# Splits of w_v and w_r made during the routed attention, parked in DRAM, and casts of x moved to ScalarE

## The chip, the core and the metric

The kernel runs on one core of a Trainium2 chip. Its engines are TensorE (PE, with the weight loads shown apart as PEld), VectorE (DVE), ScalarE (ACT) and GpSimd (POOL); SyncE (SP) issues most transfers between DRAM and the on-chip memory SBUF. Each engine works through its own queue in order; semaphores make it wait for others. The metric is the device time of one execution in microseconds (us), lower is better.

## The reference

Three stages follow each other: attention in a local window with a few global tokens (4 batches, 8 heads, 512 local and 32 global tokens, 64 wide), a mixture of 4 attention experts of which each token takes 2, and a channel mix:

```python
x_prev = concat([zeros, x[:, :-1]], axis=1)
xk = mu_k * x + (1.0 - mu_k) * x_prev
xr = mu_r * x + (1.0 - mu_r) * x_prev
k = maximum(xk @ w_k, 0.0)          # w_k is 512 x 1024
v = k * k @ w_v                     # w_v is 1024 x 512
r = 1.0 / (1.0 + exp(-(xr @ w_r)))  # w_r is 512 x 512
return r * v
```

The tokens are 4 x 576, 512 wide. Inputs of w_k, w_v and w_r arrive as 64-bit floats, so that each needs bit work before TensorE can take it.

## The kernel before, in words

A product of two fp32 matrices is made of three matmuls on a high and a low part of each operand (`mm3`). Activations and weights are therefore *split*: a cast gives the high part H, a subtraction the low part L.

The first 32 steps (n = 0 to 31) are the local attention; from step 33 on the routed attention's steps m = n - 33 run beside its end, and afterwards alone, up to m = 38 (`c_step`). A batch takes nine of them: two pairs of heads with four query blocks each, and one step for the global rows. Within a step come, in a pipeline over m, m - 1, m - 2 and m - 3, the scores (`C`, L101), their softmax on DVE and ACT (`csm`, L483 and L485), the normalisation on POOL (L501), the transposes on TensorE (`cT`, L510) with their copies out by ACT (L513) and DVE (L515, `cpt`), and the product with the values (`y`, L581). Between these, `fill` hands out groups of the projections of the next batch (`pv`, `pb..q`, `pb..k`), which need x split (`b_split`, cast L364 on DVE, subtraction L365 on POOL), and of the output projections (`po`) of the batch before.

Behind the routed attention comes the channel mix, in units of 256 tokens: mixing (`mtr`, `mmr`, `m..H`, `m..L`), eight column blocks f of `k`, each squared and split (`ksr`, `k2r`, `kk`), then `v` and `r`, and the output. Its first four blocks of `k` are made during the last batch.

The weights of the channel mix come in pieces of 128 rows x 512 columns: eight of w_k, eight of w_v (four in each half `wv0`, `wv1`), four of w_r. `load_wd` loads a piece's 512 KB into one of two `raw` buffers. `split_wd` turns it into H and L: on ACT the sign and the absolute value (L133, L134), on POOL a maximum (L136), on DVE three bit operations (L138 to L140), on ACT the cast to H (L141), on POOL the subtraction to L (L142). Its two work tiles are `wg` and `wy`, two buffers of each. H and L are written straight into tiles that earlier work uses before: w_v's first half takes the buffers of the projections' weights (`W0`, `W1`), its second half and w_r's H the `qk` buffers of the last batch, w_r's L those of w_o.

Before the change, w_k's pieces are loaded and split in steps m = 7, 10, ... 28 and the next, w_v's first half from m = 31 on, every second step, and the other eight pieces in a row behind the last output projection. w_o is split at m = 7. The order on every engine is set by a scheduler that goes by the program's order and its own estimate of when things are ready; `after(...)` keeps an instruction from being placed ahead of a given one.

## Time and profile before

| | |
|---|---|
| device time, median of 3 runs (lowest to highest) | 588.25 us (585.49 to 590.0) |
| the profiled execution: its time, its span | 588.06 us, 586.3 us |
| busy: PE, PEld | 551.9 us (94%), 458.9 us (78%) |
| busy: DVE, ACT, POOL | 342.2 us (58%), 331.1 us (56%), 315.6 us (54%) |
| mean granted clock of TensorE | 0.971 of full speed |
| moved between DRAM and SBUF | 38.72 MB, 66 GB/s over the span |

A row of the profile names a line of the kernel, an engine, an operation, and the tiles as out<-in. "Idle before" is the time in which the engine did nothing ahead of an instruction, and "<-" what ended it. Matmuls overlap, so a sum of their durations is more than their time; the distance of their starts is what counts. The granted clock is the share of TensorE's full speed that it was given in a stretch. The busy shares above are means over stages with different limits.

### The profile page before, as it was taken

How to read it: one execution, taken by the hardware profiler on the slowest of the kernel's cores; microseconds unless marked ns; L12 is line 12 of the kernel's file. 1: busy time of each engine (PE TensorE's matmuls, PEld its weight loads, DVE VectorE, ACT ScalarE, POOL GpSimd, SP SyncE). 2: the span in 40 equal slices, each digit the busy share in tenths (PEclk: the TensorE clock that was granted, in tenths of full speed). 3: DMA queues.
4: the chain of work that ended last, by engine and by line, in shares of the span. 5: the costliest groups of instructions: out<-in, count | busy, mean ns of one | idle time of the engine just before them, and what ended most of it. 6: DMA issues, size and time to landing. Idle time of an engine off the chain costs nothing. (4 is left out here: it accounts for less than half of the span.)

```text
span 586.3 us, 12786 instructions
## 1 busy us (share of the span) xinstructions
PE 551.9 (94%) x4670; PEld 458.9 (78%) x4670; DVE 342.2 (58%) x1153; ACT 331.1 (56%) x995; POOL 315.6 (54%) x416
## 2 busy tenths in 40 slices
PE   4999999999899998999998955999999999999997
PEld 2767787789788886888787833889898989898896
DVE  3768666664677487458788888864342434224211
ACT  5788775653365554365797766575444554344321
POOL 2778635352446475355688999854444443334121
PEclk9899999999899997899999986999999999999999
DMA  8998523020002110111113223000000100000000
GB/s 321 309 299 236 179 76 109 2 92 2 2 2 73 36 36 2 37 37 37 37 37 108 73 72 108 1 36 37 2 37 0 37 1 36 3 36 26 12 19 36
DMA packets 19918, 38.72 MB, mean 66 GB/s; under 512 B 9616, under 2 KB 10640, under 8 KB 19856
## 3 DMA queue, kind: packets, MB, share of 16 engines
q1 hardware_dynamic: 19280, 37.50, 19.6%
q8 instruction: 37, 0.61, 0.4%
q10 hardware_dynamic: 576, 0.41, 0.2%
q14 instruction: 25, 0.20, 0.1%
HBM read 33.45 MB, written 4.46 MB: 65 GB/s over the span
## 5 line engine op out<-in xcount | busy, mean ns | idle before, releaser
L675 POOL TENSOR_TENSOR kk<-k2r,kk 128x256 fp32r<-128x256 f32 x64 | 51.0, 800 | 78.4 <-ACT kk L674 78.4
L672 DVE TENSOR_TENSOR k2r<-ksr 128x256 f32<-128x256 f32 x64 | 34.4, 537 | 78.5 <-ACT ksr L671 74.6
L501 POOL TENSOR_TENSOR csm<-csm,crc 128x128 f32<-128x128 f32 (+3 forms) x64 | 48.7, 781 | 45.7 <-DVE crc L498 14.5
L222 ACT ACTIVATE sm<-sm,mn 128x160 f32<-128x160 f32 x128 | 53.4, 419 | 20.4 <-DVE mn L219 19.6
L655 DVE SCALAR_TENSOR_TENSOR mmr<-xT,mu,mtr 128x256 f32<-128x256 f32 (+4 forms) x96 | 52.0, 581 | 14.2 <-POOL m1L L659 6.5
L485 ACT ACTIVATE csm<-csm,cmn 128x128 f32<-128x128 f32 (+3 forms) x64 | 35.7, 559 | 30.7 <-DVE cmn L483 25.6
L671 ACT ACTIVATE ksr<-k 128x256 f32<-128x256 f32 x64 | 24.1, 379 | 44.4 <-PE k L95 44.3
L659 POOL TENSOR_TENSOR m1L<-mmr,m1H 128x256 fp32r<-128x256 f32 (+1 forms) x36 | 26.8, 757 | 32.0 <-ACT m1H L658 31.9
L654 ACT ACTIVATE mtr<-xT,omu 128x256 f32<-128x256 f32 (+4 forms) x96 | 39.7, 440 | 5.9 <-DVE mmr L655 5.1
L674 ACT CAST kk<-k2r 128x256 fp32r<-128x256 f32 x64 | 25.8, 404 | 27.4 <-DVE k2r L672 25.3
L240 POOL TENSOR_TENSOR pn<-sm,rc 128x256 f32<-128x256 f32 x64 | 37.9, 615 | 3.9 <-PE pT L259 3.0
L219 DVE CUSTOM_DVE_ANT_0 sm<-S,band 128x160 f32<-128x160 f32 x128 | 34.1, 317 | 7.3 <-PE S L209 6.3
L581 PE MATMUL y<-cpt,vC 128*64 128x128 f32 (+1 forms) x320 | 36.1, 306 | 0.7 <-DVE gsl L428 0.5
L209 PE MATMUL S<-kq 64*64 64x160 f32 x512 | 32.3, 323 | 4.3 <-DMA kq<-in_kq_dram 4.0
L93 PE MATMUL v<-wv1H,kk 128*128 128x512 f32 x68 | 27.4, 415 | 6.9 <-ACT wv1H L141 6.9
L510 PE MATMUL cT<-ident,csm 128*128 128x128 f32 x160 | 29.0, 295 | 4.7 <-DVE cpt L515 2.3
L94 PE MATMUL v<-wv1L,kk 128*128 128x512 f32 x68 | 28.1, 413 | 5.5 <-POOL wv1L L142 5.5
L244 POOL TENSOR_TENSOR glob<-sm,rc 128x128 f32<-128x128 f32 x32 | 13.0, 406 | 37.4 <-DVE rc L236 26.0
L483 DVE CUSTOM_DVE_ANT_0 csm<-C,causal 128x128 f32<-128x128 f32 (+3 forms) x64 | 29.3, 484 | 3.4 <-PE C L101 3.3
L720 DVE TENSOR_TENSOR o<-v,rt 128x512 f32<-128x512 f32 x17 | 11.6, 685 | 32.4 <-PE v L95 15.3
L365 POOL TENSOR_TENSOR x<-xT,x 128x256 fp32r<-128x256 f32 (+1 forms) x32 | 24.0, 777 | 11.9 <-DVE x L364 11.9
L581 PEld LDWEIGHTS y<-cpt,vC 128*64 128x64 f32 x320 | 22.0, 140 | 10.2 <-issue 6.0
(408 smaller groups left out, 1907.7 us busy)
## 6 DMA issues: line engine op xcount, KB each, us to landing
kq<-in_kq_dram SPq DMA_DIRECT2D x15, 688.0 KB, 4.8
vw<-in_vw_dram SPq DMA_DIRECT2D x16, 512.0 KB, 5.6
out_dram<-o SPq DMA_DIRECT2D x17, 256.0 KB, 2.0
wrawk<-in_moe_w_k_dram SPq DMA_DIRECT2D x8, 512.0 KB, 3.6
wrawv<-in_moe_w_v_dram SPq DMA_DIRECT2D x8, 512.0 KB, 3.6
wrawr<-in_moe_w_r_dram SPq DMA_DIRECT2D x4, 512.0 KB, 3.5
vgb<-in_vgd_dram SPq DMA_DIRECT2D x1, 512.0 KB, 8.3
rawwq<-in_moe_wq_dram SPq DMA_DIRECT2D x4, 128.0 KB, 9.3
```

Of the source, the lines that this page charges most:

```text
L209: nc.tensor.matmul(st[h][64 * c:64 * c + 64, i * W:(i + 1) * W], t[rr, 64 * blk:64 * blk + 64], t[rr, KT0 + 96 * blk:KT0 + 96 * blk + W], ...
L219: last_dve = nc.vector.tensor_tensor_reduce(out=ts[:, h, i], in0=st[h][:, i * W:(i + 1) * W], in1=band[:, m], op0=ALU.add, op1=ALU.min, sc ...
L222: last_act = nc.scalar.activation(ts[:, h, i], ts[:, h, i], AF.Exp, bias=mn[:, c:c + 1], scale=-1.0, accum_out=su[:, c:c + 1])
L240: nc.gpsimd.tensor_tensor(o[:, :, c], t[:, :, 96 * c:96 * c + 64], rc[:, :, None].to_broadcast([128, 4, 64]), op=ALU.mult)
L483: nc.vector.tensor_tensor_reduce(out=t[:, :w], in0=st[e][:, :w], in1=causal[:, 512 - w:], op0=ALU.add, op1=ALU.min, scale=-SCALE, scalar=B ...
L485: last_act = nc.scalar.activation(t[:, :w], t[:, :w], AF.Exp, bias=mn[:, e:e + 1], scale=-1.0, accum_out=su[:, e:e + 1])
L501: last_pool = nc.gpsimd.tensor_tensor(t[:, :w], t[:, :w], rc[:, e:e + 1].to_broadcast([128, w]), op=ALU.mult)
L581: nc.tensor.matmul(yp[64 * e:64 * e + 64, o0:o0 + n], vC[b][:, j, hh * HD:(hh + 1) * HD], pt[:, e, j, 0:n], start=j == 0, stop=j == i and ...
L654: nc.scalar.mul(mt[:, cc], xp, omu[:, kind, c:c + 1])
L655: nc.vector.scalar_tensor_tensor(mm[:, cc], x, mu[:, kind, c:c + 1], mt[:, cc], op0=ALU.mult, op1=ALU.add)
L672: nc.vector.tensor_mul(k2, s, s)
L675: nc.gpsimd.tensor_sub(hl[1], k2, v32(hl[0]))
```

## The change

1. A *jobs* list now holds w_o's load and split, then the eight pieces of w_v, the four of w_r and the eight of w_k. From m = 1 on, two of each three steps load one piece, and a split follows a step or so later; the last is done at about m = 32.
2. The pieces of w_v and w_r are split in place: H goes into the tile `wg`, L into `wy`, and both are written to a scratch in DRAM (`dr`), 256 KB each.
3. `fetch_wd` loads whole halves back into the places where they were before: w_v's first half and the H of its second at m = 30, the L of its second at m = 34, w_r behind the last output projection. A fetch is 1 MB, or two of 512 KB where the place has two buffers.
4. The cast of x in `b_split` stays on DVE for the first batch and goes to ACT for the other three.

The operations of a split, its shapes and the matmuls are the same.

```diff
-V0, VS = 31, 2
+J0, F0, F1 = 1, 30, 34
...
+    dr = ctx.enter_context(tc.tile_pool(name="dr", bufs=1, space=bass.MemoryType.DRAM))
...
+    wdr = {(name, k, s): dr.tile([128, 4, 512], F32, name=f"d{name}{k}{s}")
+           for name, k in (("v", 0), ("v", 1), ("r", 0)) for s in "HL"}
+
+    def place_wd(name, k, s):
+        tag = WD_TAG[name, k]["HL".index(s)]
+        m = 2 if tag == "wo" else 4
+        ts = [T(tag, [m, 512], f"w{name}{k}{s}{i}", F32R) for i in range(4 // m)]
+        wd.setdefault((name, k), []).append([t[:, j] for t in ts for j in range(m)])
+        return ts
+
+    def fetch_wd(name, k, s):
+        c = 0
+        for t in place_wd(name, k, s):
+            m = t.shape[1]
+            nc.sync.dma_start(v32(t), wdr[name, k, s][:, c:c + m])
+            c += m
...
+        if name == "k":
...
+            H_, L_ = [t[c % 4] for t in wd[name, k]]
+        else:
+            H_, L_ = g.bitcast(F32R), y.bitcast(F32R)
         nc.scalar.copy(H_, v32(y))
         nc.gpsimd.tensor_sub(L_, v32(y), v32(H_))
+        if name != "k":
+            for s, t in zip("HL", (H_, L_)):
+                nc.sync.dma_start(wdr[name, k, s][:, c % 4], v32(t))
...
-            nc.vector.tensor_copy(hl[0][:, c, :n], x)
+            (nc.vector.tensor_copy if b == 0 else nc.scalar.copy)(hl[0][:, c, :n], x)
...
-        if V0 <= m < V0 + 4 * VS and (m - V0) % VS == 0:
-            c = (m - V0) // VS
-            pending.append(load_wd("v", w_v, c, c // 4, 0))
-        if m >= 7 and (m - 7) % 3 == 0 and (m - 7) // 3 < 8:
-            k = (m - 7) // 3
-            pending.append(load_wd("k", w_k, k % 4, k // 4, 512 * (k // 4)))
-        if len(pending) > 1 or m >= V0 + 4 * VS - 1:
+        if jobs and m >= J0 and (m - J0) % 3 < 2:
+            pending.append(jobs.pop(0)())
+        if len(pending) > 1 or not jobs:
             for g in pending[:1]:
                 g()
             del pending[:1]
+        if m == F0:
+            for s in "HL":
+                fetch_wd("v", 0, s)
+            fetch_wd("v", 1, "H")
+        if m == F1:
+            fetch_wd("v", 1, "L")
...
+    jobs = [lambda: load_wo()]
+    jobs += [lambda c=c: load_wd("v", w_v, c, c // 4, 0) for c in range(NF)]
+    jobs += [lambda c=c: load_wd("r", w_r, c, 0, 0) for c in range(NC)]
+    jobs += [lambda c=c: load_wd("k", w_k, c % 4, c // 4, 512 * (c // 4)) for c in range(2 * NC)]
...
-    for g in pending:
-        g()
-    for c in range(4, NF):
-        load_wd("v", w_v, c, c // 4, 0)()
-    for c in range(NC):
-        load_wd("r", w_r, c, 0, 0)()
+    for s in "HL":
+        fetch_wd("r", 0, s)
```

How the change moves instructions is shown at three places. In these rows a tile's number tells copies of a tile apart, and line numbers of the changed kernel are up to 21 higher.

POOL behind the last output projection: `wy..` is a split's work tile, `w..L` a low part, `kk` and `m..` belong to the channel mix. Before:

```order
L142 TENSOR_TENSOR wv1L_5016<-wyv_5017,wv1H_5015 128x512
L136 TENSOR_SCALAR wyv_5029<-wyv_5029 128x512
L675 TENSOR_TENSOR kk<-k2r,kk 128x256
L659 TENSOR_TENSOR m0L_5117<-mmr,m0H_5116 128x256 x2
L136 TENSOR_SCALAR wyv_5041<-wyv_5041 128x512
L675 TENSOR_TENSOR kk<-k2r,kk 128x256
L142 TENSOR_TENSOR wv1L_5016<-wyv_5029,wv1H_5015 128x512
L675 TENSOR_TENSOR kk<-k2r,kk 128x256
L659 TENSOR_TENSOR m1L_5135<-mmr,m1H_5134 128x256 x2
L142 TENSOR_TENSOR wv1L_5016<-wyv_5041,wv1H_5015 128x512
L136 TENSOR_SCALAR wyv_5053<-wyv_5053 128x512
L659 TENSOR_TENSOR m1L_5135<-mmr,m1H_5134 128x256 x2
```

In the changed kernel, from the first blocks of `kk` after the routed attention on:

```order
L696 TENSOR_TENSOR kk<-k2r,kk 128x256 x2
L680 TENSOR_TENSOR m1L_4816<-mmr,m1H_4815 128x256 x4
L680 TENSOR_TENSOR m0L_5156<-mmr,m0H_5155 128x256 x4
L696 TENSOR_TENSOR kk<-k2r,kk 128x256
L680 TENSOR_TENSOR m1L_5174<-mmr,m1H_5173 128x256 x2
L696 TENSOR_TENSOR kk<-k2r,kk 128x256
L680 TENSOR_TENSOR m1L_5174<-mmr,m1H_5173 128x256 x2
L696 TENSOR_TENSOR kk<-k2r,kk 128x256
L680 TENSOR_TENSOR m_5379<-mmr,m_5379 128x256 x2
L696 TENSOR_TENSOR kk<-k2r,kk 128x256
L680 TENSOR_TENSOR m_5379<-mmr,m_5379 128x256 x2
```

The steps of the splits are gone from between the mixing and `kk`.

DVE at the cast of the fourth batch's x (`xT_87` and in the changed kernel `xT_89` are its rows; `cpt` is the copy of the transposed weights of attention), before:

```order
L385 TENSOR_TENSOR qk_2952<-pb21q_3561,qk_2952 128x288
L498 TENSOR_TENSOR crc_3623<-crc_3623,gate_2715 128x2
L364 CAST x_3629<-xT_87 128x256 x4
L515 COPY cpt_3595<-cT_3600 128x2x128
L385 TENSOR_TENSOR qk_2952<-pb21k_3580,qk_2952 128x288
L393 TENSOR_TENSOR ql<-pb21q_3561,ql 64x32
L483 ISA csm_3617,cmn_3607<-C_3609,causal 128x128
```

DVE in the changed kernel at the same copy, `128x2x128`, of the same step:

```order
L519 TENSOR_TENSOR crc_3733<-crc_3733,gate_2741 128x2
L150 SCALAR_TENSOR_TENSOR wgr_3706<-wrawr_3621,wgr_3706 128x512
L536 COPY cpt_3691<-cT_3696 128x2x128
L406 TENSOR_TENSOR qk_3016<-pb21q_3657,qk_3016 128x288
L504 ISA csm_3727,cmn_3717<-C_3719,causal 128x128
L504 ISA cmn_3717 128x1
L504 ISA csm_3730,cmn_3717<-C_3720,causal 128x128
```

And ACT in the changed kernel there:

```order
L405 CAST qk_3016<-pb21q_3657 128x288
L159 CAST wgr_3624<-wyr_3623 128x512
L405 CAST qk_3016<-pb21k_3676 128x288
L385 CAST x_3739<-xT_89 128x256 x3
L534 COPY cpt_3691<-cT_3692 128x2x128
L385 CAST x_3739<-xT_89 128x256
L413 CAST ql<-pb21q_3657 64x32
```

The four casts have left DVE, where they stood ahead of `cpt`; on ACT three of them stand ahead of its own half of that copy, and a step of a split of w_r (`wgr`) stands among the others on both engines.

SP in the changed kernel, around the first fetches (`wv1H<-dv1H` is a fetch, `wrawk` a load of a piece of w_k):

```order
L133 DMA wrawk_4167<-in_moe_w_k_dram 128x1024
L133 DMA wrawk_4352<-in_moe_w_k_dram 128x1024
L133 DMA wrawk_4432<-in_moe_w_k_dram 128x1024
L127 DMA wv1H_4663<-dv1H 128x2048
L127 DMA wv0H_4659<-dv0H 128x2048
L127 DMA wv0L_4661<-dv0L 128x2048
L133 DMA wrawk_4526<-in_moe_w_k_dram 128x1024
L133 DMA wrawk_4582<-in_moe_w_k_dram 128x1024
L133 DMA wrawk_4725<-in_moe_w_k_dram 128x1024
L127 DMA wv1L_4956<-dv1L 128x2048
L127 DMA wr0H_5147<-dr0H 128x2048
L127 DMA wr0L_5149<-dr0L 128x1024
```

Before, SP had one load behind the other there, and no write or fetch. Now three fetches of 1 MB stand ahead of the last three loads of w_k.

## Rows read from the trace of the kernel before

**Rows 1.** Busy time of each engine by stretch (start:end, length, busy us with the count of instructions for PE, PEld, DVE, ACT and POOL, then TensorE's granted clock, the DMA share and GB/s): the four batches of the routed attention, the stretch behind it, the rest.

```profile
130.00:172.00 42.00, 39.67 (x389) 34.74 (x387) 25.91 (x123) 18.95 (x59) 15.88 (x25) 0.96 0.01 2
172.00:222.00 50.00, 49.18 (x394) 40.94 (x393) 35.45 (x130) 28.25 (x83) 30.87 (x36) 1.00 0.13 43
222.00:272.00 50.00, 47.13 (x343) 39.17 (x342) 30.67 (x109) 25.03 (x72) 25.30 (x33) 0.90 0.07 22
272.00:322.00 50.00, 48.53 (x397) 38.48 (x396) 41.56 (x130) 38.88 (x111) 38.28 (x43) 1.00 0.20 64
340.00:382.00 42.00, 28.06 (x137) 21.73 (x136) 35.39 (x47) 27.71 (x68) 39.22 (x32) 0.80 0.21 63
382.00:586.00 204.00, 200.54 (x1161) 177.00 (x1159) 73.47 (x139) 89.48 (x239) 75.59 (x104) 1.00 0.06 23
```

**Rows 2.** TensorE's waits from 322 to 386 us: who waited for whom, us in total, times, longest.

```profile
PE v L93 <- ACT wv1H L141: 6.9, 3, 3.5
PE v L94 <- POOL wv1L L142: 5.5, 4, 3.0
```

**Rows 3.** The chain of waits from 338 to 382 us, shares by line.

```profile
by line: DVE wgr L139 11.9%; DVE mmr L655 9.3%; POOL wyv L136 8.4%; POOL wv1L L142 8.2%; POOL kk L675 8.2%; DVE wyr L140 7.6%; DVE wyr L138 7.5%; issue 7.2%; DVE wyv L140 5.1%; POOL m0L L659 4.6%; DVE wyv L138 4.2%; POOL wyr L136 3.7%; POOL
```

**Rows 4.** Busy time from 340 to 382 us of the instructions that touch `v`, then `k`, then `r` (columns as in rows 1, engines that have none left out).

```profile
340.00:382.00 42.00, 10.30 (x24) 5.44 (x24) 0.00 (x0) 0.80 0.21 63
...
340.00:382.00 42.00, 12.78 (x90) 12.55 (x88) 3.28 (x9) 0.80 0.21 63
...
340.00:382.00 42.00, 7.12 (x23) 4.16 (x24) 0.00 (x0) 0.80 0.21 63
```

**Rows 5.** TensorE in order of time (start, duration, line): two neighbours of `v`, and two of `k`, in undisturbed stretches.

```profile
387.68 0.39 PE L93 MATMUL v<-wv0H,kk 128*128 128x512 f32 x1
387.90 0.39 PE L94 MATMUL v<-wv0L,kk 128*128 128x512 f32 x1
...
338.03 0.28 PE L93 MATMUL k<-m,wk1H 128*128 128x256 f32 x1
338.15 0.28 PE L94 MATMUL k<-m,wk1H 128*128 128x256 f32 x1
```

**Rows 6.** The steps of a split: groups by line from 130 to 322 us, on POOL and on DVE (busy us, mean ns of one | idle us before them and what ended it), then single lines over the whole span (duration ns min/median/max) on POOL and on ACT.

```profile
L136 POOL TENSOR_SCALAR wyk<-wyk 128x512 f32<-128x512 f32 x8 | 11.9, 1484 | 1.6 <-ACT wyk L134 1.6
...
L142 POOL TENSOR_TENSOR wk1L<-wyk,wk1H 128x512 fp32r<-128x512 f32 x4 | 5.2, 1288 | 5.2 <-DVE crc L498 3.6 <-ACT wk1H L141 1.6
L142 POOL TENSOR_TENSOR wk0L<-wyk,wk0H 128x512 fp32r<-128x512 f32 x4 | 5.1, 1274 | 15.7 <-ACT wk0H L141 12.1 <-DVE crc L498 3.6
...
L136 POOL TENSOR_SCALAR wyv<-wyv 128x512 f32<-128x512 f32 x3 | 4.4, 1485 | 0.3 <-ACT wyv L134 0.3
...
L142 POOL TENSOR_TENSOR wv0L<-wyv,wv0H 128x512 fp32r<-128x512 f32 x1 | 1.3, 1287 | 0.1
...
L140 DVE SCALAR_TENSOR_TENSOR wyk<-wyk,wgk 128x512 uint32<-128x512 uint32 x8 | 6.9, 860 | 0.0
...
L138 DVE TENSOR_SCALAR wyk<-wyk 128x512 uint32<-128x512 uint32 x8 | 4.6, 580 | 0.6 <-POOL wyk L136 0.6
...
L136 POOL TENSOR_SCALAR wyr<-wyr x4: 1656/1920/1924, 358.0 to 374.0; 128x512 f32<-128x512 f32 x4
...
L142 POOL TENSOR_TENSOR wv1L<-wyv,wv1H x4: 1266/1490/1709, 340.5 to 359.9; 128x512 fp32r<-128x512 f32 x4
...
L133 ACT ACTIVATE wgk<-wrawk,tcol x8: 738/744/761, 181.6 to 296.6; 128x512 f32<-128x512 f32 x8
...
L134 ACT ACTIVATE wyk<-wrawk x8: 647/658/672, 182.2 to 297.3; 128x512 f32<-128x512 f32 x8
...
L141 ACT CAST wk0H<-wyk x4: 609/620/623, 188.5 to 244.7; 128x512 fp32r<-128x512 f32 x4
```

**Rows 7.** DVE's first step of a split (L139) in the second and the fourth batch: busy us and count, then clock and DMA as in rows 1.

```profile
172.00:222.00 50.00, 2.08 (x3) 1.00 0.13 43
272.00:322.00 50.00, 3.80 (x6) 1.00 0.20 64
```

**Rows 8.** TensorE's waits from 130 to 340 us, as in rows 2.

```profile
PE cT L510 <- POOL csm L501: 1.2, 3, 0.5
```

**Rows 9.** The casts of x on DVE over the whole span; then, in order of time, DVE and TensorE in the third batch, and an ACT cast of the same size.

```profile
L364 DVE CAST x<-xT x32: 275/596/1343, 56.5 to 264.3; 128x256 fp32r<-128x256 f32 x16, 128x288 fp32r<-128x288 f32 x16
...
223.41 4.16 DVE L364 CAST x<-xT 128x256 fp32r<-128x256 f32 x4
...
228.05 0.88 PE L510 MATMUL cT<-ident,csm 128*128 128x128 f32 x3 [2.32 <-DVE cpt L515]
...
365.20 0.39 ACT L658 CAST m<-mmr 128x256 fp32r<-128x256 f32 x1
```

**Rows 10.** Two stretches of 10 us in the third batch, columns as in rows 1.

```profile
220.00:230.00 10.00, 7.44 (x52) 5.98 (x53) 8.37 (x22) 4.56 (x15) 6.01 (x7) 0.88 0.00 0
230.00:240.00 10.00, 10.00 (x51) 7.84 (x52) 4.69 (x16) 3.38 (x10) 3.92 (x7) 0.61 0.07 13
```

**Rows 11.** The transfer rate in 40 slices of the span, and two loads (KB each, us from issue to landing).

```profile
GB/s 321 309 299 236 179 76 109 2 92 2 2 2 73 36 36 2 37 37 37 37 37 108 73 72 108 1 36 37 2 37 0 37 1 36 3 36 26 12 19 36
...
kq<-in_kq_dram SPq DMA_DIRECT2D x15, 688.0 KB, 4.8
...
wrawk<-in_moe_w_k_dram SPq DMA_DIRECT2D x8, 512.0 KB, 3.6
```

More of the change, by code (lines that the diff above doesn't have):

```diff
@@ L119, in split_wd @@
     def split_wd(name, raw, c, k):
-        if (name, k) not in wd:
-            wd[name, k] = []
-            for s, tag in zip("HL", WD_TAG[name, k]):
-                m = 2 if tag == "wo" else 4
-                ts = [T(tag, [m, 512], f"w{name}{k}{s}{i}", F32R) for i in range(4 // m)]
-                wd[name, k].append([t[:, j] for t in ts for j in range(m)])
-        H_, L_ = [t[c % 4] for t in wd[name, k]]
         lo, hi, hf = raw[:, :, 0], raw[:, :, 1], v32(raw)[:, :, 1]
@@ L140, in split_wd @@
         nc.vector.scalar_tensor_tensor(y, y, 0x7f800000, g, op0=ALU.bitwise_xor, op1=ALU.bitwise_xor)
+        if name == "k":
+            if (name, k) not in wd:
+                for s in "HL":
+                    place_wd(name, k, s)
+            H_, L_ = [t[c % 4] for t in wd[name, k]]
+        else:
+            H_, L_ = g.bitcast(F32R), y.bitcast(F32R)
         nc.scalar.copy(H_, v32(y))
         nc.gpsimd.tensor_sub(L_, v32(y), v32(H_))
+        if name != "k":
+            for s, t in zip("HL", (H_, L_)):
+                nc.sync.dma_start(wdr[name, k, s][:, c % 4], v32(t))
     wqk, wraw = {}, {}
@@ L346, in load_wo, with split_wo @@
         nc.sync.dma_start(raw, wo.rearrange("(a e) d m -> (e d) a m", a=2))
-        wraw["o"] = raw
-    def split_wo():
+        return lambda: split_wo(raw)
+    def split_wo(raw):
         with after(last_act):
-            nc.scalar.copy(woS[0], wraw["o"])
+            nc.scalar.copy(woS[0], raw)
         with after(last_pool):
-            nc.gpsimd.tensor_sub(woS[1], wraw["o"], v32(woS[0]))
+            nc.gpsimd.tensor_sub(woS[1], raw, v32(woS[0]))
     xHL, qk, vC, gate, lg = {}, {}, {}, {}, {}
@@ L770, in c_step @@
             d_k(0, m - K0)
-        if m == 7:
-            split_wo()
-        if V0 <= m < V0 + 4 * VS and (m - V0) % VS == 0:
-            c = (m - V0) // VS
-            pending.append(load_wd("v", w_v, c, c // 4, 0))
-        if m >= 7 and (m - 7) % 3 == 0 and (m - 7) // 3 < 8:
-            k = (m - 7) // 3
-            pending.append(load_wd("k", w_k, k % 4, k // 4, 512 * (k // 4)))
-        if len(pending) > 1 or m >= V0 + 4 * VS - 1:
+        if jobs and m >= J0 and (m - J0) % 3 < 2:
+            pending.append(jobs.pop(0)())
+        if len(pending) > 1 or not jobs:
             for g in pending[:1]:
@@ L849, in chain_kernel @@
             c_step(n - CS)
-    load_wo()
     for m in range(NU + 6 - CS, NCU + 3):
@@ L855, in chain_kernel @@
         g()
-    for g in pending:
-        g()
-    for c in range(4, NF):
-        load_wd("v", w_v, c, c // 4, 0)()
-    for c in range(NC):
-        load_wd("r", w_r, c, 0, 0)()
+    for s in "HL":
+        fetch_wd("r", 0, s)
     for n, (g0, w) in enumerate(tokens):
```

## The prediction

> **What bounds the kernel now.** I read the stretches first, then TensorE's waits, then the chain of waits, then the single steps. The rows of [rows 1] give six stretches: the routed attention's four batches (130 to 322 us of the span, some 48 us each), 340 to 382 us, and the rest. In the batches TensorE is busy 39.67 of 42, 49.18 of 50, 47.13 of 50 and 48.53 of 50 us: it bounds them, with little idle time. From 340 to 382 it is busy 28.06 of 42 us at a granted clock of 0.80 of full, while DVE (35.39) and POOL (39.22) are nearly full. That is the one stretch with another limit; behind it the engines other than TensorE are less than half busy.
>
> What ends TensorE's waits there stands in [rows 2]: `v` on the cast `wv1H` (6.9 us) and on the subtraction `wv1L` (5.5): 12.4 us together, on pieces of w_v in the making. The chain of waits says the same [rows 3]: from 338 to 382 us its largest shares are DVE's and POOL's steps of the splits (`wgr`, `wyv`, `wv1L`, `wyr`) and their mixing, and no matmul is among the lines it names. These eight splits begin after the last output projection, when nothing else is left to cover them.
>
> **The change, part by part.** The profiled run took 588.06 us for a span of 586.3; the median of the runs is 588.25, so they agree within 0.2 us. I make the sum against 588.06.
>
> *(a) The eight splits of w_v's second half and w_r leave 340 to 382 us.* What stays there for TensorE is 24 `v`, 23 `r` and 90 `k` matmuls [rows 4]. Undisturbed, a 512-column one starts 0.22 to 0.23 us after the one before it, a 256-column one 0.12 us [rows 5]: 47 x 0.23 + 90 x 0.12 = 10.8 + 10.8 = 21.6 us instead of 42. **Minus 20.4 us**, waits and lowered clock together. What could be late next: DVE, ACT and POOL keep their mixing and `kk` work. POOL's is about 39.2 less eight pairs of split steps (8 x 2.8 to 3.2 us) = 14 to 17 us [rows 1, 6], under 21.6, so TensorE stays the bound.
>
> *(b) The four splits of w_v's first half leave 305 to 337 us.* TensorE idles 50 - 48.53 = 1.47 us in the fourth batch [rows 1]; 1.2 us of its waits from 130 to 340 are for POOL's `csm` [rows 8]. Between nothing and 1.5 us, half: **minus 0.7**.
>
> *(c) All twelve, with the eight of w_k, now fall in steps 1 to 32 of the routed attention.* Each issues three steps on ACT (0.744 + 0.658 + 0.620 = 2.0 us), two on POOL (1.48 + 1.28 = 2.8) and three on DVE (0.69 + 0.58 + 0.86 = 2.1) [rows 6]. There were 11 splits in 130 to 322 us (w_k's eight, three of w_v), now 20: 9 more, so ACT +18, POOL +25, DVE +19 us over 192 us, in which they were busy 111, 110 and 134 (the sums over the four batches) [rows 1]. No engine fills up. The price is the delay of the steps queued behind. The nearest rows are the second and fourth batch: three splits by DVE's first step of each, with 0.82 us of TensorE idle, and six with 1.47 [rows 1, 7], or 0.22 us a split; 9 x 0.22 = **plus 2.0**. The ends are 0 (hidden) and one more stall of the size of (d), 7.1.
>
> *(d) 24 casts of x move from DVE to ACT.* On DVE the median is 0.60 us; an ACT cast of 128x256 takes 0.39 [rows 9]. Off DVE go 24 x 0.60 = 14 us, which nearly pays for its 19 of (c); ACT gets 9.4 more. At one place the casts are on the path: at 223.41 DVE spends 4.16 us on four of them, the transpose's copy `cpt` stands behind, and TensorE waits 2.32 us for that [rows 9]; the granted clock is then 0.88 and 0.61 [rows 10], which costs 0.12 x 7.44 + 0.39 x 10 = 4.8 us, 7.1 in all. In the changed order DVE's copy stands ahead of this work, but ACT's half of the same copy stands behind three casts (1.2 us). Between 0 and 7.1 I take the wait and a little of the clock, **minus 3.0**.
>
> The row has casts of 0.28 us and of 1.34 us, of nearly the same size [rows 9]. The Trainium skill (SBUF — State Buffer, "SBUF: two separate sides") says that a DVE cast in a two-port mode and a POOL instruction lock each other out for the whole instruction, while ACT has ports of its own. By that rule POOL gains with DVE and all of the 7.1 us goes: the sum would be 562.4 instead of 566.5. The 4.16 us for four casts agrees with it, but TensorE's next wait is POOL's, which the trace doesn't show without the casts, so I stay with the row.
>
> *(e) The transfers.* 24 writes and seven loads go onto SP's queue. SP has nothing but transfers there, so their issue delays only transfers. Bound from below: 0. The place where they can matter is the fetch of w_v, below as a rival: between 0 and its 9.4 us, and near the lower end, since the first slice is the nearest row for large loads side by side; in the sum **plus 0.5**. w_r's low part waits for the two `wo` buffers, free after the last output projection. From there to the first `r` matmul the changed order has 30 `v` and 44 `k` matmuls: 30 x 0.23 + 44 x 0.12 = 12.2 us, against 3.6 us for a load of 512 KB [rows 11]. Cost nothing while that cover stands; without it, some 4 us.
>
> *(f) w_o's split, earlier by some steps, and the smaller allocation changes:* the same instructions; nothing.
>
> Sum: 588.06 - 20.4 - 0.7 + 2.0 - 3.0 + 0.5 = **566.5 us**. The ends of the terms: 588.06 - 20.4 - 1.5 - 7.1 = 559; 588.06 - 20.4 + 7.1 + 4 = 579.
>
> **The rivals.**
>
> *1. A fetch holds up w_k.* On SP, 1 MB each of `wv0H` and `wv0L` stands right ahead of the load of w_k's sixth piece, and waits until the last projection of the fourth batch frees the two buffers. In the changed ACT order the cast that shows this moment stands 18 instructions ahead of the step that needs the piece; at the fourth batch's pace of 111 instructions in 50 us that is 8.1 us. The load lies behind 2 MB, 2.5 MB in all: 8.2 us at the 321 GB/s of the first slice, or 17.5 at what 176 KB more cost between the two loads (1.2 us, 150 GB/s) [rows 11]. ACT would stand still for 0.1 to 9.4 us, and behind it the copies that TensorE waits for. At the long end 566.5 + 9 = **575.5**. For it: no slack; against: the rate of large loads side by side should be near the first slice's. Chance 0.12.
>
> *2. Half of the gain stays away.* The chain `k`, ACT, DVE, ACT, POOL, `v` with the mixing of the next tokens takes the place of the splits: POOL at up to 17 us and DVE need only one badly placed mix. Without half of (a): 566.5 + 10.2 = **577**. Chance 0.07. Against: from 382 us on TensorE runs this very loop without such a wait, with POOL busy 75.6 of 204 us [rows 1].
>
> *3. POOL's queue becomes the bound: slower.* POOL runs in order and sits between two halves of a split until DVE and ACT are through. In 130 to 322 us it idled 1.6 + 5.2 + 15.7 = 22.5 us ahead of w_k's steps, 2.8 us per split [rows 6]. Its other work there is 110.3 - 27.9 (the split rows) = 82.4 us. Twenty splits at 2.8 us of work and 2.8 of waiting make 112 + 82 = 194 us, just over the 192 of the stretch; the point from which it decides is 2.7 us of waiting a split. With the steps at 3.6 us, as beside full engines (1.92 + 1.71, the longest [rows 6]), it is 211, 19 us too long, and if the clock follows as in the third batch (2.87 us idle, 4.7 us lost to the 0.90 clock [rows 1]) up to 50. That gives 585 to 617, say **600**. For it: the numbers above; against: POOL sat there with nothing else to do, TensorE waited 1.2 us for its `csm` in all [rows 8], and the changed order puts other POOL work between the halves. Chance 0.06.
>
> The Trainium skill (SBUF — State Buffer, "Who interferes with whom") also has a rule against the change: a DVE instruction with two SBUF inputs, like two of the split's three, and a POOL instruction that reads SBUF block each other. By it DVE's 20 x 2.1 = 43 us would come on top of POOL's 82 + 56, leaving some 11 us of room instead of 54, an estimate from this trace's durations; 0.6 us of waiting a split would then do for rival 3. POOL's step that grows from 1.48 to 1.92 us beside a full DVE agrees with it.
>
> *4. The batches gain more than I count*, all of (b) and (d) with (c) at nothing: 559 or less. Chance 0.04.
>
> That the change doesn't do what it says I leave at nothing: the order has no split behind the routed attention.
>
> **The numbers.** The forecast, 566.5 us, holds 0.71 of the chance; the range 558 to 579 holds it with rivals 1 and 2 and the upper part of rival 4, leaving out rival 3 and tails. One per cent, about what a measurement of this kernel can tell from no change, is 582.4 us on the fast side. Faster: forecast, rivals 1, 2, 4 but for tails, 0.90. Within 1%: 0.05, rival 3's lower end and tails. Slower: 0.05.
>
> **What would show it.** (a) No wait of `v` or `r` for `wv1H`, `wv1L` or `wr0H`; granted clock 1.0 over the forty us after the last `po`; TensorE busy throughout, and the first output some 20 us earlier. (c) Each batch within 2 us of its 48; waits for POOL's `csm` still small. (d) No 2 us wait for `cpt` in the third batch, its clock above 0.90. (e) No ACT wait for the sixth `wrawk`, none of TensorE for `wr0L`. I am wrong if the batches together last over 200 us, or if TensorE idles over 5 us after the last `po`.

## The result, and the profile after

The changed kernel took **568.32 us** (median of 4 runs, 564.63 to 573.91) beside 588.2 us for the kernel before: a ratio of **0.9645, 95% interval [0.9572, 0.9718]**, faster by 3.6%. Ratios here leave out a run over 1.5% above the fastest of its kernel, such as that of 573.91 us. The profiled run took 566.68 us for a span of 564.9. The forecast was 566.5 us.

The stretches of the changed kernel, columns as in [rows 1]:

```profile
130.00:172.00 42.00, 40.29 (x403) 34.99 (x403) 29.46 (x126) 25.70 (x76) 22.69 (x28) 1.00 0.20 64
172.00:222.00 50.00, 48.85 (x388) 40.73 (x387) 42.83 (x128) 36.03 (x100) 42.55 (x45) 1.00 0.41 137
222.00:272.00 50.00, 48.10 (x391) 41.41 (x389) 40.91 (x131) 34.99 (x98) 39.37 (x41) 1.00 0.34 108
272.00:322.00 50.00, 43.48 (x361) 36.03 (x360) 44.56 (x122) 38.35 (x106) 40.55 (x44) 0.97 0.37 136
340.00:382.00 42.00, 42.00 (x250) 37.39 (x249) 21.01 (x41) 24.89 (x68) 19.54 (x27) 1.00 0.07 26
```

From 340 to 382 us TensorE is busy throughout, at full clock, where it had 28.06 us at 0.80 [rows 1]. In the batches its idle time (length less busy) was 2.3, 0.8, 2.9 and 1.5 us and is now 1.7, 1.2, 1.9 and 6.5: the third batch got better and the fourth much worse.

The chain of waits from 338 to 382 us named DVE's and POOL's split steps [rows 3]. From 340 to 382 us it now reads:

```profile
by line: PE k L96 12.9%; PE k L95 12.9%; PE k L94 12.8%; PE v L94 12.0%; PE v L95 12.0%; PE v L96 12.0%; PE r L95 8.6%; PE r L94 8.6%; PE r L96 8.6%
```

Matmuls alone. TensorE's four largest waits from 100 to 400 us in the changed kernel, as in [rows 2]:

```profile
PE po L94 <- DVE cpt L536: 3.6, 1, 3.6
PE y L602 <- ACT cpt L534: 2.2, 2, 1.3
PE pv L94 <- ACT x L385: 2.1, 2, 1.9
PE k L94 <- DVE cmn L504: 1.2, 1, 1.2
```

No `v` or `r` waits for a weight any more. At the head stands a new wait, in the fourth batch, for DVE's copy `cpt`.

The last output projection divides the span in two. Its last matmul, before and after, in order of time:

```profile
331.85 0.29 PE L95 MATMUL po<-ytH,woL 128*128 128x272 f32 x1
```
```profile
330.11 0.29 PE L96 MATMUL po<-ytH,woL 128*128 128x272 f32 x1
```

Before, 586.3 - 331.85 = 254.45 us lay behind it, now 564.9 - 330.11 = 234.8. So **19.65 us were gained behind it and 1.74 ahead of it**. That small second number is what the experiments had to take apart.

Two things blur it. Eight fewer `k` matmuls stand ahead of the last output projection in the changed kernel (52 for 60, 1.0 us), so that at equal work 20.6 us were gained behind it and 0.8 ahead. And the start differs from one execution to the next. The last score matmul `S` of the local attention, which has the same 1608 matmuls ahead of it in every kernel here, started at 120.7 us before and at 122.5 after:

```profile
L209 PE MATMUL S<-kq x512: 296/296/527, 4.0 to 120.7; 64*64 64x160 f32 x171
```
```profile
L230 PE MATMUL S<-kq x512: 296/296/527, 4.0 to 122.5; 64*64 64x160 f32 x171
```

So the distance from this `S` to the last output projection is the fairer measure of the batches. It is 211.2 us before and 207.6 after, 3.6 less, of which the eight `k` make 1.0.

DVE ahead of that late copy in the fourth batch (start, duration, line), and POOL at the same time:

```profile
293.44 0.95 DVE L149 TENSOR_SCALAR wyk<-wyk 128x512 uint32<-128x512 uint32 x1 [0.28 <-POOL wyk L147]
294.43 1.10 DVE L151 SCALAR_TENSOR_TENSOR wyk<-wyk,wgk 128x512 uint32<-128x512 uint32 x1
295.45 1.31 DVE L676 SCALAR_TENSOR_TENSOR mmr<-xT,mu,mtr 128x256 f32<-128x256 f32 x1
296.69 0.57 DVE L517 TENSOR_SCALAR crc<-csu 128x2 f32<-128x2 f32 x1
297.17 0.55 DVE L536 COPY cpt<-cT 128x384 f32<-128x384 f32 x1
...
293.38 1.60 POOL L680 TENSOR_TENSOR m<-mmr,m 128x256 fp32r<-128x256 f32 x2
294.95 1.54 POOL L571 TENSOR_TENSOR pl<-pl,lrc 128x544 f32<-128x544 f32 x1
296.46 1.66 POOL L147 TENSOR_SCALAR wyk<-wyk 128x512 f32<-128x512 f32 x1
```

Two steps of a split of w_k and one of the channel mix's mixing, with a short `crc`, stand ahead of `cpt`, and TensorE idles 3.60 us for it.

### The profile page after: what moved, and what is told of

Its sections match the earlier page's. It is cut to its first block, busy times and chain, and to the rows that moved or that the text cites. A ratio compares the mean times of both kernels' runs of the same rounds, so it can differ in the third digit from the quotient of the medians.

```text
span 564.9 us, 12840 instructions
## 1 busy us (share of the span) xinstructions
PE 541.0 (96%) x4670; PEld 455.4 (81%) x4670; DVE 329.1 (58%) x1129; ACT 337.5 (60%) x1019; POOL 312.6 (55%) x416
## 4 chain that ended last, share of the span: by engine, by line
PE 81%; DVE 11%; ACT 3%; POOL 2%; DMA 1%; issue 1%; ACTq 0%; DVEq 0%; POOLq 0%
PE v L94 6%; PE v L95 5%; PE v L96 5%; PE k L96 5%; PE k L95 5%; PE k L94 5%; PE S L230 4%; PE x L348 3%; PE pT L280 3%; PE y L602 3%; PE r L94 3%; PE r L95 3%; PE r L96 3%; PE C L102 2%; PE cT L531 2%; PE po L94 2%
## 5 line engine op out<-in xcount | busy, mean ns | idle before, releaser
L696 POOL TENSOR_TENSOR kk<-k2r,kk 128x256 fp32r<-128x256 f32 x64 | 48.6, 762 | 83.3 <-ACT kk L695 83.2
L693 DVE TENSOR_TENSOR k2r<-ksr 128x256 f32<-128x256 f32 x64 | 30.6, 478 | 88.2 <-ACT ksr L692 84.3
L522 POOL TENSOR_TENSOR csm<-csm,crc 128x128 f32<-128x128 f32 (+3 forms) x64 | 52.8, 846 | 28.3 <-DVE crc L519 16.0
L676 DVE SCALAR_TENSOR_TENSOR mmr<-xT,mu,mtr 128x256 f32<-128x256 f32 (+4 forms) x96 | 53.9, 599 | 16.6 <-POOL m0L L680 5.7
L680 POOL TENSOR_TENSOR m1L<-mmr,m1H 128x256 fp32r<-128x256 f32 (+1 forms) x36 | 26.4, 744 | 42.4 <-ACT m1H L679 37.9
L602 PE MATMUL y<-cpt,vC 128*64 128x128 f32 (+1 forms) x320 | 31.1, 296 | 2.3 <-ACT cpt L534 2.2
L230 PEld LDWEIGHTS S<-kq 64*64 64x64 f32 x512 | 20.7, 142 | 12.5 <-issue 4.2
L679 ACT CAST m1H<-mmr 128x256 fp32r<-128x256 f32 (+1 forms) x36 | 13.4, 391 | 25.5 <-DVE mmr L676 13.2
L102 PE MATMUL C<-qk 64*128 64x128 f32 (+3 forms) x192 | 28.4, 351 | 0.1
L348 PE MATMUL x<-pt,vw 128*64 128x64 f32 x512 | 28.2, 233 | 0.0
```

Source lines behind the costliest of these rows:

```text
L102: nc.tensor.matmul(op[0], op[a], op[x], start=n == 0, stop=n == 2)
L230: nc.tensor.matmul(st[h][64 * c:64 * c + 64, i * W:(i + 1) * W], t[rr, 64 * blk:64 * blk + 64], t[rr, KT0 + 96 * blk:KT0 + 96 * blk + W], ...
L348: nc.tensor.matmul(xs[pp][rr, 64 * blk:64 * blk + 64], w, pt[2 * pp + m // 2][:, 2 * h + m % 2, 64 * c:64 * c + 64], start=blk == 0, stop= ...
L522: last_pool = nc.gpsimd.tensor_tensor(t[:, :w], t[:, :w], rc[:, e:e + 1].to_broadcast([128, w]), op=ALU.mult)
L602: nc.tensor.matmul(yp[64 * e:64 * e + 64, o0:o0 + n], vC[b][:, j, hh * HD:(hh + 1) * HD], pt[:, e, j, 0:n], start=j == 0, stop=j == i and ...
L676: nc.vector.scalar_tensor_tensor(mm[:, cc], x, mu[:, kind, c:c + 1], mt[:, cc], op0=ALU.mult, op1=ALU.add)
```

## The experiments

Theory A: the gain is the 20 us behind the last output projection, and the batches come out even. Theory B: the casts of x are a good part of it. The rivals blame POOL's or ACT's queue. C and D were formed for the fourth batch after the first results. All spans below are those of profiled runs, "last po" is the start of the last output projection's last matmul. The marks explained above, for the kernels that the account below rests on:

| kernel | last `S` | last po | between them | behind last po |
|---|---|---|---|---|
| before | 120.7 | 331.85 | 211.2 | 254.4 |
| before, casts on ACT | 122.9 | 323.19 | 200.3 | 254.0 |
| changed, three profiles | 122.5, 122.9, 121.3 | 330.11, 333.14, 328.82 | 207.6, 210.3, 207.5 | 234.8 in each |
| changed, casts on DVE | 122.7 | 337.10 | 214.4 | 234.7 |
| changed, without the twelve | 123.4 | 327.95 | 204.5 | 234.9 |
| only eight parked | 120.3 | 321.46 | 201.1 | 238.7 |

**The changed kernel again**, with no edit, twice, as a yardstick beside the other kernels.

> The changed kernel once more, beside the others. Theory A (the gain is the 20 us of the stretch behind the last output projection, and the four batches come out even): 566 to 569 us, ratio 0.96 to 0.97; TensorE without a pause for 40 us behind the last po, and a pause of some 3.5 us at 294 to 298 us for DVE's copy cpt. Theory B (a good part of the gain is the casts of x that left DVE): the same time, told apart by the next two runs.

> The changed kernel again, beside the next two on the same chip. 566 to 574 us as in the two runs of it so far; the last output projection starts 330 to 333 us into the span, and from there to the end it is 234.8 us.

Measured: 573.35 us, ratio 0.9719 [0.9672, 0.9765], last po at 333.14 and 234.8 us behind it; then 565.69, 0.9642 [0.9593, 0.9691], 328.82 and 234.8. What lies behind is the same to 0.1 us; what lies ahead moves by 4 us from one execution to the next, 1.6 of it ahead of the last `S`. The third batch of the first profile (220 to 230 and 230 to 240 us, columns as in [rows 1]):

```profile
220.00:230.00 10.00, 8.14 (x66) 6.78 (x66) 8.58 (x35) 7.41 (x25) 5.29 (x5) 1.00 0.44 122
230.00:240.00 10.00, 9.96 (x79) 8.64 (x79) 8.73 (x23) 6.67 (x16) 10.00 (x14) 1.00 0.41 142
```

and of the repeat:

```profile
220.00:230.00 10.00, 7.89 (x62) 6.57 (x63) 8.34 (x32) 7.40 (x27) 5.49 (x5) 0.96 0.38 99
230.00:240.00 10.00, 10.00 (x59) 7.82 (x58) 7.17 (x19) 5.16 (x13) 9.97 (x13) 0.70 0.47 163
```

The same stall, 1.9 us at 227 us in the first and 2.1 at 228 in the second: `pv` waits for the cast of x, which now stands in ACT's queue. Behind it the granted clock stayed at 1.00 in one execution and fell to 0.70 in the other. A stall of this size is a risk for the clock. The spread of this kernel's times goes with the clock too: its runs went from 564.5 at a mean clock of 0.993 to 575.8 at 0.973. Where the clock fell in the slower ones is not shown, since the profiles are of the faster ones.

**The eight splits alone**: the kernel before, without the splits of w_v's second half and w_r. Their places are loaded from a scratch that holds other weights.

```diff
-    for c in range(4, NF):
-        load_wd("v", w_v, c, c // 4, 0)()
-    for c in range(NC):
-        load_wd("r", w_r, c, 0, 0)()
+    for name, k in (("v", 1), ("r", 0)):
...
+                nc.sync.dma_start(v32(t), scr[:, i * m:i * m + m])
```

> The kernel before without the eight splits behind the last output projection: the second half of w_v and w_r are not computed, their places are loaded from a scratch that holds parts of the experts' q weights. Theory A: the whole gain, 566 to 569 us, ratio 0.962 to 0.968, TensorE busy 42 of the 42 us behind the last po. Theory B: 573 us or more. Rival (another chain takes the splits' place, mixing and kk): 575 to 580 us with waits of v for kk behind the last po.

Measured: 571.23 us, 0.9699 [0.9662, 0.9736]; last po at 331.30, 237.1 us behind it. From 340 to 382 us, and TensorE's only wait from 330 to 400:

```profile
340.00:382.00 42.00, 40.44 (x230) 35.39 (x229) 21.48 (x40) 26.25 (x70) 22.64 (x30) 1.00 0.04 14
...
PE v L93 <- ACT kk L676: 1.6, 1, 1.6
```

The eight splits were worth 254.45 - 237.1 = 17.35 us. At equal work it is 18.4, since two `v` and five `k` matmuls (1.1 us) that stood ahead of last po before now stand behind it. The time lies between theory A's (566 to 569) and B's (573 or more), and the rival's wait is there, but short: `v` waits 1.6 us for `kk`, which the changed kernel doesn't do.

**The casts**: alone in the kernel before, and taken out of the changed one.

```diff
-            nc.vector.tensor_copy(hl[0][:, c, :n], x)
+            (nc.vector.tensor_copy if b == 0 else nc.scalar.copy)(hl[0][:, c, :n], x)
```

> The kernel before with only the casts of x of batches two to four moved to ACT. Theory A: 583 to 586 us, ratio 0.991 to 0.997; the 2.3 us wait for cpt in the third batch is gone and its granted clock above 0.95, the stretch behind the last output projection is unchanged (42 us for 21 us of matmuls). Theory B: 575 to 581 us, ratio under 0.988.

> The changed kernel with all casts of x back on DVE. Theory A, with the price of the prediction for the casts (3 us): 569 to 572 us, ratio to the kernel before 0.968 to 0.975, with a longer wait of TensorE for cpt or x in one batch. Theory B, also by the page's rule that DVE's casts and POOL lock each other out: 573 to 580 us, DVE and POOL steps longer in every batch. If the casts are worth nothing: within 1 us of the changed kernel.

Measured: alone 579.66 us, 0.9837 [0.9801, 0.9873], last po at **323.19**, 8.66 us earlier than before, and 254.0 us behind it, as before. Its batches:

```profile
130.00:172.00 42.00, 40.78 (x408) 35.45 (x408) 24.99 (x123) 22.84 (x71) 15.64 (x25) 1.00 0.01 3
172.00:222.00 50.00, 49.85 (x400) 41.66 (x397) 33.24 (x122) 30.55 (x93) 30.72 (x37) 1.00 0.14 43
222.00:272.00 50.00, 49.95 (x410) 42.02 (x409) 33.38 (x128) 31.13 (x96) 30.37 (x38) 1.00 0.11 33
272.00:322.00 50.00, 48.96 (x386) 39.29 (x387) 41.90 (x110) 38.99 (x105) 41.04 (x45) 1.00 0.20 64
```

The third batch went from 47.13 us at 0.90 to 49.95 at 1.00: the stall and its clock are gone as a whole. The first batch gained too (0.96 to 1.00). From the last `S` on, 10.9 us were gained. Taken out of the changed kernel, the casts moved last po to 337.10, 4 to 8 us later (4 to 7 from the last `S` on); by the times it is not told apart (574.08, 0.9745 [0.9712, 0.9778], beside 573.35 measured with it), within the 1 us that was expected if the casts are worth nothing. Theory B holds for the kernel before; in the changed kernel the casts are worth less, and the times don't show how much.

**The twelve splits taken out**, with their loads and writes; w_k's eight stay at the end of the list, and the fetches read a scratch with other weights.

```diff
-    jobs += [lambda c=c: load_wd("v", w_v, c, c // 4, 0) for c in range(NF)]
-    jobs += [lambda c=c: load_wd("r", w_r, c, 0, 0) for c in range(NC)]
+    jobs += [lambda: lambda: None for c in range(NF + NC)]
```

> The changed kernel without the twelve splits of w_v and w_r, their loads and their writes; the fetches stay and read a scratch that holds parts of the experts' q weights, so v and r are not the reference's. Theory A (the four batches lose to what stands together in the fourth: w_k's splits and the mixing on DVE): the fourth batch keeps its 4 to 6 us of TensorE idle, the first three win 1 to 2 us, 564 to 567 us. Rival (the twelve splits are the price): the idle time goes in all batches, 557 to 561 us.

Measured: 565.3 us, 0.9598 [0.9568, 0.9628]; last po at 327.95. The second and third batches are nearly without idle time (0.15 and 0.00 us), the first keeps its 1.7, and the fourth its stall:

```profile
222.00:272.00 50.00, 50.00 (x408) 42.32 (x406) 33.84 (x119) 30.63 (x92) 27.92 (x34) 1.00 0.17 54
272.00:322.00 50.00, 43.27 (x355) 35.46 (x357) 42.63 (x114) 37.12 (x104) 40.38 (x44) 0.97 0.32 117
...
PE po L94 <- DVE cpt L535: 3.6, 1, 3.6
```

The 3.6 us stall stays without the twelve. So it doesn't hang on them; ahead of the copy stand w_k's own steps, which the change moved to the end of the list, beside the mixing. The twelve have a price too, in the other batches: from the last `S` to last po 204.5 us here and 207.5 or 207.6 with them, 3 us, and 5.8 where the clock fell. By the times (0.9598 [0.9568, 0.9628] and, measured apart, 0.9642 to 0.9719 for the changed kernel) it is not clear of noise.

**Which queue is it?** In three kernels one step of all 20 splits is done twice: POOL's maximum, DVE's first three-operand step, ACT's absolute value.

```diff
+            nc.gpsimd.tensor_scalar(v32(y), v32(y), TINY, None, op0=ALU.max)
```
```diff
+        nc.vector.scalar_tensor_tensor(g, lo, 29, g, op0=ALU.logical_shift_right, op1=ALU.bitwise_or)
```
```diff
+            nc.scalar.activation(v32(y), hf, AF.Abs)
```

> The changed kernel with POOL's maximum of each split done twice (the second changes nothing): 20 x 1.5 = 30 us more POOL work in the batches. Theory A (POOL has room): up to 4 us slower than the changed kernel, 567 to 571 us. Rival POOL (the third rival of the prediction: POOL's queue is near its bound): 10 to 30 us slower, 577 us and more, with TensorE waiting for csm.

> The changed kernel with DVE's first step of each split done twice (the second changes nothing): 20 x 0.7 to 1.0 = 14 to 20 us more DVE work. Theory A (DVE is the queue that holds up TensorE in the fourth batch): 5 to 10 us slower, 572 to 577 us, with longer waits for DVE's cpt and csm there. Rival POOL: at most 2 us slower, 567 to 569 us.

> The changed kernel with ACT's absolute value of each split done twice: 20 x 0.66 = 13 us more ACT work. Theory A: 0 to 3 us slower, 567 to 570 us. Rival ACT (with the casts of x, ACT is now the queue that TensorE waits for): 5 us or more, 572 us and above, with waits for ACT's x and cpt.

| doubled | added work, 20 steps | last po | time, ratio |
|---|---|---|---|
| POOL | 1.5 us each, 30 us | 329.68 | 571.31, 0.9702 [0.9668, 0.9736] |
| DVE | 0.69 to 0.93 us each, 14 to 18 us | **341.56** | **579.21, 0.9832 [0.9794, 0.9871]** |
| ACT | 0.67 us each, 13 us | 333.38 | 568.4, 0.9642 [0.9603, 0.9681] |

The changed kernel's last po was at 329 to 333. Thirty more us on POOL leave it there, as do 13 on ACT; 14 to 18 on DVE put it 8 to 13 us later. DVE's queue is the sensitive one, POOL's has room in the batches. Behind last po the kernel with POOL doubled takes 238.6 us, 3.8 more than the changed one, of which 0.9 are `k` and `v` matmuls that moved behind it.

The doubled step also makes the scheduler order other work anew, so that these kernels don't tell where a queue is tight. With POOL doubled the fourth batch lost its stall, and with DVE doubled the wait for `cpt` there became shorter (1.9 us), not longer as expected; what DVE's work cost shows in the second and third batches. The fourth batch with POOL doubled, the third with DVE doubled:

```profile
272.00:322.00 50.00, 47.65 (x377) 37.81 (x375) 43.01 (x128) 37.07 (x103) 44.55 (x45) 0.97 0.50 169
```
```profile
222.00:272.00 50.00, 45.27 (x338) 37.33 (x338) 40.08 (x124) 32.51 (x91) 38.45 (x39) 0.94 0.34 106
```

**Where the last splits stand**: the same 20 splits, in three of four steps, or in each.

```diff
-        if jobs and m >= J0 and (m - J0) % 3 < 2:
+        if jobs and m >= J0 and (m - J0) % 4 < 3:
```
```diff
-        if jobs and m >= J0 and (m - J0) % 3 < 2:
+        if jobs and m >= J0:
```

> The changed kernel with a piece in three of four steps of the routed attention in place of two of three: the same 20 splits in the batches, the last three done before the mixing of the channel mix stands in DVE's queue; in the order on DVE only one step of the mixing is left ahead of the copy cpt for which TensorE waited 3.6 us. Theory C (the place of the last splits beside the mixing costs the fourth batch, not their number): that stall falls below 1.5 us, TensorE is busy over 46 of 50 us in the fourth batch (43.5 in the changed kernel), the last output projection starts at 325 to 328 us, 3 to 5 us below the changed kernel in the same call. Theory D (each split in the batches costs its share wherever it stands): the fourth batch gains what the earlier ones lose, the last output projection starts at 329 to 334, and the time is within 2 us of the changed kernel.

> The changed kernel with a piece in each step: all 20 splits are done by the end of the third batch, none beside the mixing. Theory C: the fourth batch is as good as in the kernel before (48.5 us busy) or better, but DVE and POOL have nine splits in one batch, where they were 36 to 43 us busy of 50 with six; the second and third batches lose 1 to 3 us each by that, so 327 to 331 us to the last output projection, within 3 us of the changed kernel. Theory D: as three_of_four, 329 to 334 us. If the density decides, both lose: over 335 us.

Measured: 573.23 us, 0.9756 [0.9714, 0.9799], last po 336.82; and 575.76, 0.9805 [0.976, 0.985], 339.75. Both slower than the changed kernel measured with them (565.69, 0.9642 [0.9593, 0.9691]). Of three of four, the first, the third and the fourth batch, and three of TensorE's waits:

```profile
130.00:172.00 42.00, 37.65 (x353) 33.29 (x353) 25.54 (x112) 22.91 (x65) 21.44 (x25) 0.88 0.16 52
...
222.00:272.00 50.00, 46.34 (x342) 38.65 (x341) 39.24 (x117) 33.03 (x90) 34.32 (x34) 0.90 0.34 106
272.00:322.00 50.00, 46.52 (x397) 38.50 (x395) 46.03 (x146) 39.33 (x114) 40.48 (x48) 1.00 0.36 127
...
PE pv L94 <- ACT x L385: 3.7, 2, 3.2
PE gl L480 <- DVE gb L473: 2.6, 1, 2.6
...
PE po L94 <- DVE cpt L536: 0.6, 1, 0.6
```

Theory C was right on the fourth batch (the wait is 0.6 us, TensorE busy 46.52 at full clock) and wrong on the time: stalls of 2.6 us in the first batch and 3.2 in the third took its place, with clocks of 0.88 and 0.90. Theory D gave 329 to 334, too early. What came out is the third case, that density decides: with more splits per step there are stalls elsewhere. That it is the density, and not the new order that came with it, is argued from two kernels and not shown.

**Only eight parked**: w_v's first half is split into its places in steps 31 to 37, as before; the density stays at two of three.

```diff
-    jobs += [lambda c=c: load_wd("v", w_v, c, c // 4, 0) for c in range(NF)]
+    jobs += [lambda c=c: load_wd("v", w_v, c, c // 4, 0) for c in range(4, NF)]
...
+        if V0 <= m < V0 + 4 * VS and (m - V0) % VS == 0:
+            c = (m - V0) // VS
+            pending.append(load_wd("v", w_v, c, 0, 0))
```

> The changed kernel with only eight pieces parked (w_v's second half and w_r); w_v's first half is split into its places in steps 31 to 37, as in the kernel before. Two of three steps still take a piece, so the first three batches hold as many splits as in the changed kernel, the last is done some five steps earlier, and three of w_v's fall at the end of the fourth batch. Behind the last output projection 234.5 to 235.5 us as in the changed kernel. If what the batches lose is a matter of a few stalls of TensorE and of the lowered clock behind each, set by which steps meet in DVE's queue: no stall of 3.6 us for cpt in the fourth batch, TensorE busy over 47 of 50 us there at a clock of 1.0, the first three batches as in the changed kernel to 1.5 us, the last output projection at 323 to 327 us, and 559 to 563 us. If w_v's first half is better parked, as the prediction's term (b) has it: 0.7 to 1.5 us more than that, still below the changed kernel. If the order meets with new stalls in the first three batches, as in the two kernels before this one: each shows as a wait of over 2 us with a clock below 0.95 in the same batch, and the time is 568 us or more.

Measured: 565.56 us (561.97 to 570.18), 0.9607 [0.955, 0.9664]; last po at **321.46**, but 238.7 us behind it. The fourth batch, and 340 to 382 us with TensorE's wait there:

```profile
272.00:322.00 50.00, 48.36 (x410) 40.09 (x409) 42.41 (x118) 40.26 (x114) 41.58 (x45) 1.00 0.24 82
...
340.00:382.00 42.00, 40.06 (x243) 36.11 (x242) 18.18 (x36) 24.35 (x65) 19.70 (x26) 0.96 0.07 26
...
PE v L94 <- ACT kk L695: 1.9, 1, 1.9
```

The fourth batch is whole again, with the first three as in the changed kernel: the expectation for the batches held. The one for what follows (234.5 to 235.5 us) didn't: `v` waits 1.9 us for `kk` and the clock falls. Of the 8.65 us gained ahead of last po (6.5 from the last `S` on), 3.9 are given back behind it. Its profiled span, 560.2 us, is the shortest of all, but its interval overlaps that of the changed kernel's best series (0.9642), so it isn't shown to be faster.

## Why the prediction was right, and which steps were not

The sum, 566.5, lay within 0.2 us of the profiled run and 2 of the median (7 and 1 of the medians of the two repeats). But two of its terms were wrong by 5 us and more, in opposite directions.

**What bounds it, and (a).** Right. The stretch from 340 to 382 us is full at clock 1.0, and `r` began 12.3 us after the last output projection (330.11), where 12.2 were worked out:

```profile
342.44 0.39 PE L94 MATMUL r<-wr0H,m1H 128*128 128x512 f32 x1
```

The eight splits alone gave 17.35 us of the 20.4; with (b)'s four 19.65, or 20.6 at equal work.

**(b), minus 0.7 in the batches.** Not shown there: no kernel takes this term alone. Both kernels that split w_v's first half late and have the rest of the gain (before without the eight, and only eight parked) wait 1.6 to 1.9 us for `kk` behind the last output projection, and take 2.3 and 3.9 us longer there than the changed kernel. That parking it saves these is not shown: the two kernels differ in other things too, with only eight parked no split is left beside the wait, and the kernel with POOL doubled, which parks all twelve, loses TensorE's time there as well (`k` waits 1.8 us for `rt`).

**(d), minus 3.0.** The failed step was the choice of "the wait and a little of the clock" between 0 and 7.1: the casts alone gave **8.7 us**, 10.9 from the last `S` on. By the rows of the batches, the third gained 2.8 us of idle time and about 4.7 of clock (0.10 x 47), so the whole of the 7.1, and the first 1.1 and about 1.6 (0.04 x 40). The first batch's part was left out of the sum: [rows 8] shows one of TensorE's waits from 130 to 340 us, and two larger ones stand beside it, the one of 2.3 us for `cpt` and this one in the first batch, with casts of x ahead of it in DVE's queue:

```profile
PE gl L459 <- DVE crc L496: 1.8, 1, 1.8
```

In the kernel before, the stall in the third batch went without a successor; in the changed kernel `pv` waits 1.9 us for the cast on ACT at nearly the same place. The measured gain alone is nearer to the 7.1 that the prediction worked out by the Trainium skill (SBUF — State Buffer, "SBUF: two separate sides") than to the 3.0 of the row I stayed with. That doesn't test the rule: the casts' leaving the queue ahead of `cpt` would by itself end the stall.

**(c), plus 2.0.** The failed step was to price the splits by their number alone and to leave "one more stall of the size of (d)" at the end of the term. From the casts alone to the changed kernel, last po moves from 323.19 to 330.11: **6.9 us** (7.3 from the last `S` on), most in the fourth batch (48.96 us busy to 43.48, clock 1.00 to 0.97). Without the twelve, 4.2 of the 7.3 are left: they stay with w_k's eight splits, whose number is the same and whose place is new. The twelve make the other 3 us or so, 0.26 a split, so the price of 0.22 was near for these. The stall hangs on the place: with twelve fewer splits it is 3.6 us all the same, and with the last ones elsewhere (only eight parked) it is gone.

So (b), (c) and (d) were put at -1.7 us together and came to -1.7 ahead of last po, as +6.9 and -8.7, or to -3.6 from the last `S` on, as +7.3 and -10.9. That is luck, not a reading. Nor do the two terms stand alone: taken in the other order, the splits first, they are +3.2 (the changed kernel with its casts on DVE) and -4 to -7.

**(e).** Right that no fetch or load is waited for: the fetches of 1 MB landed in 4.7 to 6.7 us, w_k's loads in 3.6 as before, and neither ACT nor `r` waited for one. What ACT did wait for is a write, which holds a `wy` buffer until it has landed; the sum has nothing for that, and no run shows what it cost:

```profile
wrawk<-in_moe_w_k_dram SPq DMA_DIRECT2D x8, 512.0 KB, 3.6
...
wv0L<-dv0L SPq DMA_DIRECT2D x1, 1024.0 KB, 6.7
...
wr0L<-dr0L SPq DMA_DIRECT2D x2, 512.0 KB, 4.2
...
ACT wyr L145 <- DMA dv1L<-wyv: 1.2, 1, 1.2
```

**The rivals.** 1 did not happen. 2 did not happen here, but its mechanism, the chain through `kk`, is what the kernel with only eight parked meets at 1.9 us. 3 is refuted: it gave 585 us and more, TensorE waited 0.5 us for POOL's `csm`, and POOL bore 30 us more in the batches. It put the danger on the wrong engine; DVE, which the sum relieved by 14 us and loaded with 19, is the one that makes TensorE wait. 4 happened for (d) and failed for (c).

**What would have shown it.** (a), (d) and (e) came as announced, and the batches stayed below 200 us; "each batch within 2 us of its 48" failed in the fourth.

## What to carry over

Price work that is slipped in between by the places where TensorE's next input stands in the same engine's queue, not by the engine's idle share or by a mean per piece: here 3.6 us hung on a few instructions ahead of one copy. When a sum of small terms comes out, test the terms alone; two large ones can hide in it. Give the point that you measure from the same work on both sides, and check that the start is the same: 1.8 us of difference ahead of the batches hid half of what they gained. And look at which other stall a cure moves: in the kernels that thinned out the fourth batch, stalls stood in the first and third.

## What the runs showed of the hardware

DVE's split steps grew in the changed kernel, w_k's first step most. L139 of the kernel before, and the same one in the changed kernel (L150), over the batches (busy us, mean ns of one):

```profile
L139 DVE SCALAR_TENSOR_TENSOR wgk<-wrawk,wgk 128x512 uint32<-128x512 uint32 x8 | 5.5, 691 | 0.4
```
```profile
L150 DVE SCALAR_TENSOR_TENSOR wgk<-wrawk,wgk 128x512 uint32<-128x512 uint32 x8 | 8.4, 1048 | 0.2
```

The same eight instructions take half as long again; w_v's eight take 0.76 us and w_r's four 0.69. The longest, with the POOL step at its side:

```profile
287.84 1.78 DVE L150 SCALAR_TENSOR_TENSOR wgk<-wrawk,wgk 128x512 uint32<-128x512 uint32 x1
...
287.79 1.29 POOL L160 TENSOR_TENSOR wk1L<-wyk,wk1H 128x512 fp32r<-128x512 f32 x1 [1.35 <-ACT wk1H L159]
```

It begins just behind POOL's subtraction and ends 0.54 us behind that one's end. The rows ahead of the late copy in the fourth batch look alike: L151 took 1.10 us and ended 0.55 us behind POOL's L680, and the mixing step took 1.31 and ended 0.27 behind POOL's L571 (shortest of their kind from 130 to 322 us: 0.68 and 0.47). Together they took 1.3 us more than their shortest, a good part of the 3.60 that TensorE idled. POOL's maximum there took 1.66, where its mean was 1.48 before [rows 6]. The prediction priced DVE's steps at 2.1 us a split; they took 2.5. The casts of x before look like this too: the four at 223.41 us [rows 9] took 1.34, 1.13, 1.12 and 0.80 us, and each ended some 0.15 us behind the POOL instruction that was running when it began; the shortest took 0.28.

The Trainium skill (SBUF — State Buffer, "Who interferes with whom") says that a DVE instruction with two SBUF inputs and a POOL instruction that reads SBUF contend. These rows beside POOL's two-input steps agree. Not all do: at 190.85 us an L150 took its usual 0.69 us wholly beside POOL's maximum (190.31 to 191.80). Here it was mostly DVE's queue that paid, not POOL's, as the prediction's rival 3 had it.

The granted clock, last: the same stall of about 2 us near 227 us left it at 1.00 in one execution and took it to 0.70, a mean between its two levels, in another, and that span was 3.0 us longer.
